# Attention and token-mixing MLP on one core: the order of instructions from a search over partial orders, with the dispatcher's tolerances set for each stretch of the program

## The chip, the cores and the metric

The kernel runs on one core of one Trainium2 chip. The metric is the device time in microseconds (us) of one execution. A core has five engines with a queue of instructions each: TensorE (PE in the profile; its weight loads are shown apart as PEld), VectorE (DVE), ScalarE (ACT), GpSimd (POOL) and SyncE (SP), which here issues DMAs. Each engine works its queue strictly in the order in which the program was written; across engines only semaphores order the work.

## The reference

The input is normalized once, and the result goes through a 32-head attention and through an MLP over the token axis; both are added to the input. Cut to what matters:

```python
S, D, H, Dh, F = 2048, 512, 32, 16, 1376
def _A_ref(x, wqkv, wo):
    q, k, v = split_heads(x @ wqkv)
    p = _softmax(einsum("bhqd,bhkd->bhqk", q, k) * Dh ** -0.5)
    return merge_heads(einsum("bhqk,bhkd->bhqd", p, v)) @ wo

def _B_ref(x, w1, b1, w2, b2):
    h = _layernorm(x)
    u = _gelu(einsum("bsd,sf->bdf", h, w1) + b1)
    return transpose(einsum("bdf,fs->bds", u, w2) + b2)

xn = _layernorm(A_x)
return A_x + _A_ref(xn, A_wqkv, A_wo) + _B_ref(xn, B_w1, B_b1, B_w2, B_b2)
```

The largest part by far is the softmax: 32 heads x 2048 x 2048 exponentials.

## The kernel before

**Tiling.** Attention is cut into 32 blocks (`NBLK`): 4 blocks of 512 queries times 8 sets of 4 heads. A block has 16 groups, one for each tile of 128 keys, 512 groups in all (`NGRP`). A group is 4 score rows, one for each head: a 128 x 512 tile of scores, which TensorE makes with one matmul (`score_mm`, L558) into one of eight PSUM banks. The 4 heads lie in 4 row groups of the array, so matmuls for different heads run side by side.

**Two ways to an exponential.** ScalarE takes two score rows at a time from a pair of banks (banks 0 and 1, or 2 and 3, by turns) with one exponential over 1024 columns into a buffer `pT` (`exp_tile`, L566); a group is two of those. VectorE makes its exponentials with integer arithmetic on the bits of a bf16: for each score row a first pass (`dve_first`, L613) from bank 4, 5 or 7 into a plane in SBUF, an add and a clamp; then two more planes for the whole group (`add_plane`, L618), each the first plane shifted by a constant. The three planes are summed by TensorE. So a group costs ScalarE two instructions, or VectorE six. Planes live in `plx` and in tiles that are done with (`x_sb`, `xn_sb`, part of `h_sb`, and others).

**PV.** `pv_mm` (L578) multiplies the exponentials by V and sums over the key tiles in bank 6; an extra column of ones gives the softmax's denominator. A PV bundle is 4 matmuls in 4 column groups of the array: one bundle for a group of ScalarE, three (one for each plane) for a group of VectorE. When a block's last bundle is done, its epilogue (`chain_epi`) copies bank 6 (L1095), takes the reciprocals (L1110) after a trip through DRAM, broadcasts them by DMA and multiplies on GpSimd (L1132). The last block has a shorter epilogue on VectorE (`tail_epilogue`: transposes L1737 and L1744), followed by its half of the output projection (L909) and four stores.

**Everything else** is cut into chains of steps: the projections of K, V and Q (L499), the MLP's first product (L860, with L871 to empty the bank), the GELU on ScalarE in the midst of the exponentials (L882, with two loads of activation tables), the MLP's second product with the output projection of finished blocks (L891, L901), and the normalizations. These matmuls use the full array and run in bank 7, 5 or 4 while no score row of VectorE is there.

**What sets the order.** Nothing is ordered by hand behind the ramp. A dispatcher runs on the host while the program is built: it keeps a planned clock for each engine (`Sched.add` adds a planned duration and end for each instruction, and 95 ns, `SWITCH`, when TensorE changes between score rows, PV columns and full-array matmuls) and asks the engine with the earliest clock for its next piece of work. That order becomes the engines' queues; semaphore waits are derived from the tiles read and written. On the chip nothing is decided again. `pe_step` chooses for TensorE:

- If ScalarE's next pair of banks is free within reach, it issues two score rows for it, and along with them score rows for VectorE into banks that are free within `JOIN` (80 ns).
- Otherwise it lets `pe_fill` issue a filler: a PV bundle, or the next full-array matmul of a chain. A filler may end up to `TOL` (115 ns) behind the moment at which ScalarE's banks come free.
- `DEFER` (250 ns) is how far it puts the score rows off so that a VectorE bank can come free and join them.
- If VectorE's backlog is under `D_HUNGRY` (0), or ScalarE's banks are over `FAR` (1300 ns) away, it issues score rows for VectorE alone.
- If fewer than `KEEP` (8) units of work stand in the last 3.4 us of the plan, it issues a matmul of zeros (L1579).

`dve_step` chooses for VectorE by priority: emptying a bank of a chain, first passes (`P1_PRI`, -1, when all three banks are taken), then planes (2). `D_PEND` (0) is how many score rows of VectorE's may be pending before another group is fetched. Which groups go to VectorE isn't fixed in advance; `d_pick1` gives it the next open group whenever score rows can be issued for it, so the split follows from the plan.

Of the kernel before, what the change touches and what calls it, by code (L numbers as in the profile page):

```python
# [1 line left out]

# [11 lines left out]
S = 2048  # L14
# [43 lines left out]
NPB = 8  # L58
# [25 lines left out]

SWITCH = 95.0


class Sched:  # L90
    ENGS = ("pe", "act", "dve", "pool", "sp")

    def __init__(self, nc, es):
        self.nc = nc
        self.es = es
        self.streams = {e: [] for e in self.ENGS}
        self.order = []
        self.last_writer = {}
        self.readers = {}
        self.dma_ops = []  # L100
        self.free = {e: 0.0 for e in self.ENGS}
        self.cfg = None
        self.busy = {e: 0.0 for e in self.ENGS}
        self.two = None
        self.wide = 0.0

    def ready(self, reads=(), writes=(), eng=None):
        t = 0.0
# [13 lines left out]
    def add(self, eng, fn, reads=(), writes=(), name="", dma=False, extra_deps=(), out_dma=False,  # L122
            occ=100.0, lat=None, cfg=None, two=False):
        op = Op(eng, fn, name)
        op.is_dma = dma
        op.q = "o" if out_dma else "i"
        deps = set()
        for k in reads:
            w = self.last_writer.get(k)
            if w is not None:  # L130
                deps.add(w)
            if k[0] == "bank":
                for r in self.readers.get(k, ()):
# [12 lines left out]
        if eng == "pe" and not dma:  # L146
            deps = {d for d in deps if d.eng != "pe" or d.is_dma}
        op.deps = list(deps)
        for k in reads:
            self.readers.setdefault(k, []).append(op)  # L150
        for k in writes:
            self.last_writer[k] = op
            self.readers[k] = []
        op.pos = len(self.streams[eng])
        self.streams[eng].append(op)
        self.order.append(op)
        if dma:
            self.dma_ops.append(op)
        t = self.free[eng]
        if cfg is not None:  # L160
            if self.cfg is not None and cfg != self.cfg:
                t += SWITCH
            self.cfg = cfg
        if eng == "pool" and self.two is not None:
            op.deps.append(self.two)
        for d in op.deps:
            t = max(t, d.end)
        if two:
            t = max(t, self.wide)
            self.two = op  # L170
        op.start = t
        op.occ = occ
        op.end = t + (lat if lat is not None else occ + 150.0)
        self.free[eng] = t + occ
        if eng == "pool" and occ > 1000.0:
            self.wide = t + occ
        self.busy[eng] += occ
        return op
# [79 lines left out]
def bass_parallel_sum__softmax_full_mha__mixer_token_mlp__prompt_kernel(  # L258
# [18 lines left out]
    with ExitStack() as es:  # L277
# [65 lines left out]
        def dma(q, dst, src, reads, writes, name="", noncontig=False, out_dma=False, lat=2500.0, move=150.0):  # L343
            if noncontig:
                def fn(eng, dst=dst, src=src):
                    with nc.allow_non_contiguous_dma(reason="small strided transfer"):
                        return eng.dma_start(dst, src)
            else:
                def fn(eng, dst=dst, src=src):
                    return eng.dma_start(dst, src)  # L350
            op = sc.add(q, fn, reads=reads, writes=writes, name=name, dma=True, out_dma=out_dma, occ=450.0, lat=lat)

            dma_free[0] = max(dma_free[0], op.start + 1300.0) + move
            op.end = max(op.end, dma_free[0] + 700.0)
            return op

        NPRE = 4
# [363 lines left out]
        plane_busy = {}  # L721
        pv_block = [0]
        pv_open = [True]
        kt_done = {0: 4}
        vt_done = {0: 4}
        k0_done = set(range(NPRE))
# [22 lines left out]
        class Chain:  # L749
# [6 lines left out]

            def pace(self):
                n = sum(s.eng == "pe" for s in self.steps)
                return self.rel + (self.due - self.rel) * self.i / n - 0.05

            def head(self):
                return self.steps[self.i] if self.i < len(self.steps) else None
# [678 lines left out]
                    bg[-1].t = sc.streams["pe"][-1].end  # L1441
                    bg[-1].due = -1.0

        TOL = 115.0
        JOIN = 80.0
        DEFER = 250.0
        P1_PRI = -1
        D_PEND = 0

        def pe_fill(t, lim, same_cfg):  # L1450
            cands = []
# [7 lines left out]
            for xb in (EX_BANK, 5, 4):  # L1459
# [15 lines left out]
                if ch is not None and ch.head().eng == "pe" and ch.t <= t:  # L1475
                    if rdy is None:
                        rdy = [c for c in ex_queue if c.rel <= st_["pos"] and (c.gate is None or c.gate())]
                    if any(c is not ch for c in rdy) or ch.pace() <= st_["pos"] or (early and xb != EX_BANK):
                        if not any(c[0] == "F" and ex_active[c[2]] is None for c in cands) or early:
                            cands.append(("F", ch, xb))  # L1480
                        late = late or ch.due < st_["pos"]
            order = []
            pv_press = len(buf_busy) >= NPB - 3 or len(planes_avail()) < 3
            for c in cands:
                same = 0 if c[0] == sc.cfg else 1
                if sc.cfg == "S" and n_unit(c, t) < 2:
                    same = 2
                if c[0] == "P":
                    order.append(((0 if pv_press else 1), same, 0.0, c))
                else:  # L1490
                    order.append(((0 if late else 1), same, c[1].due, c))
            order.sort(key=lambda z: z[:3])
            for _, _, _, c in order:
                if same_cfg and c[0] != sc.cfg:
# [110 lines left out]
        def act_left():  # L1605
            return sum(groups_open.values()) + len(act_cur[1])

        D_HUNGRY = 0.0
        PVM, PLM, PAM = 0.0, 0.0, 0.0
        FAR = 1300.0  # L1610
        n_act_ = [0]

        def chain_step(ch, t):
# [16 lines left out]
        def dve_step(t):  # L1630
# [20 lines left out]
            pool_on = sc.wide > t  # L1651
            for dg in d_groups:
                if dg["n1"] == 4 and dg["t"] <= t and not pool_on and plane_room(dg):
                    c.append((0.5 if closing(dg) else 2, dg["g"], lambda dg=dg: plane_step(dg)))
            if not c:
                return False
            min(c, key=lambda z: z[:2])[2]()
# [24 lines left out]
            return False  # L1682

        def wake_times(t):
            z = []
            for o in sc.order[-400:]:
                if o.end > t:
                    z.append(o.end)
                if o.start > t:
                    z.append(o.start)  # L1690
            for v in sc.free.values():
                if v > t:
                    z.append(v)
            return min(z) if z else None

        sc.free["sp"] = 0.0
        look = {e: sc.free[e] for e in ("pe", "dve", "pool", "sp")}
        guard = 0
        while True:
# [4 lines left out]
            if t > look[e]:  # L1704
                look[e] = t
                continue
            now[0] = t
            if e == "pe":
                did = pe_step(t)
            elif e == "dve":  # L1710
# [134 lines left out]
```

## Time and profile before

| | us |
|---|---|
| three runs | 696.21, 696.72, 697.99 (median 696.72) |
| the profiled execution | 697.93 |
| its span, first to last instruction | 696.1 |
| ScalarE busy | 679.5 |
| VectorE busy | 656.5 |
| TensorE busy (matmuls) | 655.3 |
| GpSimd busy | 66.3 |

The profile is that of one execution. Busy times count the stretches in which at least one instruction of an engine is under way; neighbours on an engine overlap, so the mean duration of an instruction is longer than what it adds to the end, and the pitch (from start to start) is the better price. "L566" is line 566 of the kernel before; the changed kernel has the same code further down (L566 is its L649, L558 its L641, L613 and L618 its L696 and L701, L578 its L661). DMA traffic is light: 41 GB/s from and to HBM over the span.

### The profile page before, as it was taken

The numbers are of one execution on the slowest core, as the hardware profiler recorded it, in microseconds if no ns is written. First come the engines' busy times: TensorE is split into PE (matmuls) and PEld (weight loads), VectorE is DVE, ScalarE is ACT, GpSimd is POOL, SyncE is SP. The second block draws the span as 40 slices with busy tenths as digits, with TensorE's granted clock in tenths as the row PEclk, the third lists the DMA queues.
The fourth block names the chain that finished last, engine by engine and source line by source line (L and its number), as shares of the span: only waits on it lengthen the run. The fifth ranks groups of instructions, "written<-read, shape, count | busy, mean of one in ns | idle before, by whom it ended". The sixth has DMA issues, their size and how long they took to land.

```text
span 696.1 us, 15540 instructions
## 1 busy us (share of the span) xinstructions
PE 655.3 (94%) x6195; PEld 199.7 (29%) x6281; DVE 656.5 (94%) x1139; ACT 679.5 (98%) x741; POOL 66.3 (10%) x94
## 2 busy tenths in 40 slices
PE   8999999999999999999999999998989999999987
PEld 4533333322222222222222222222222222222222
DVE  6988999999999999999999999999999999999997
ACT  5999999999999999999999999999999999999995
POOL 5520100000000000000000000000000000002000
PEclk9999999999999999999999999999999999999999
DMA  8042100112122312102221222211110022211001
GB/s 214 29 81 40 37 14 14 28 49 52 41 55 52 72 30 53 40 19 56 58 59 46 54 52 54 54 44 45 41 26 15 24 53 63 55 45 43 11 14 46
DMA packets 78431, 32.65 MB, mean 47 GB/s; under 512 B 63068, under 2 KB 74268, under 8 KB 78360
## 3 DMA queue, kind: packets, MB, share of 16 engines
q1 hardware_dynamic: 77512, 31.27, 18.5%
q8 instruction: 49, 0.80, 0.5%
q10 hardware_dynamic: 848, 0.39, 0.2%
q14 instruction: 22, 0.18, 0.1%
HBM read 26.08 MB, written 2.61 MB: 41 GB/s over the span
## 4 chain that ended last, share of the span: by engine, by line
ACT 85%; PE 10%; DVE 4%; issue 1%; DMA 0%; DVEq 0%; SPq 0%
ACT pT L566 83%; PE ps L558 3%; PE ps L578 3%; PE ps L891 1%; PE ps L499 1%; DVE x_sb L613 1%; ACT gT L882 1%; DVE stats L444 1%; PE ps L901 1%; PE ps L632 0%; DMA x_sb<-in_A_x_dram 0%; DVE plx L613 0%; DVE xnT L495 0%; DVE xn_sb L464 0%; PE ps L909 0%
## 5 line engine op out<-in xcount | busy, mean ns | idle before, releaser
L566 ACT ACTIVATE pT<-ps 128x1024 bf16<-128x1024 f32 x726 | 666.6, 1146 | 1.3 <-PE ps L558 0.9
L558 PE MATMUL ps<-QT,KT 32*128 32x512 bf16 x2048 | 289.2, 384 | 20.9 <-ACT pT L566 17.5
L613 DVE TENSOR_SCALAR x_sb<-ps 128x512 int16<-128x512 f32 x292 | 198.8, 683 | 14.2 <-PE ps L558 4.4
L613 DVE TENSOR_SCALAR plx<-ps 128x512 int16<-128x512 f32 x260 | 169.6, 679 | 1.3 <-PE ps L558 0.9
L558 PEld LDWEIGHTS ps<-QT,KT 32*128 32x128 bf16 x2048 | 73.4, 91 | 277.7 <-ACT pT L566 267.0
L578 PE MATMUL ps<-pT,V 128*32 128x512 bf16 x1452 | 142.8, 390 | 0.8 <-DVE OT L1095 0.4
L618 DVE TENSOR_SCALAR x_sb<-plx 128x2048 int16<-128x2048 int16 x88 | 59.7, 682 | 1.4 <-PE ps L578 0.8
L578 PEld LDWEIGHTS ps<-pT,V 128*32 128x32 bf16 x1452 | 36.2, 93 | 79.8 <-issue 75.0
L578 PE MATMUL ps<-x_sb,V 128*32 128x512 bf16 x580 | 56.0, 382 | 0.8 <-issue 0.5
L618 DVE TENSOR_SCALAR plx<-x_sb 128x2048 int16<-128x2048 int16 x74 | 50.5, 685 | 2.7 <-PE ps L578 2.5
L578 PE MATMUL ps<-plx,V 128*32 128x512 bf16 x544 | 52.8, 382 | 0.3 <-DVE plx L613 0.3
L1132 POOL TENSOR_TENSOR oT<-OT,denb 128x512 bf16<-128x512 f32 x16 | 20.3, 1268 | 340.5 <-DVE x_sb L618 166.0
L891 PE MATMUL ps<-gT,w2blk 128*128 128x512 bf16 (+1 forms) x150 | 48.2, 384 | 3.3 <-issue 2.9
L860 PE MATMUL ps<-h_sb,w1blk 128*128 128x512 bf16 (+1 forms) x158 | 47.9, 385 | 2.6 <-issue 2.2
L618 DVE TENSOR_SCALAR x_sb<-x_sb 128x2048 int16<-128x2048 int16 x65 | 44.1, 681 | 0.2
L1132 POOL TENSOR_TENSOR otmp<-OT,denb 128x512 bf16<-128x512 f32 x15 | 19.1, 1271 | 261.5 <-DVE x_sb L618 168.0
L499 PE MATMUL ps<-xnT,wqkv_sb 128*128 128x512 bf16 (+1 forms) x166 | 35.3, 309 | 3.0 <-issue 1.9
L578 PE MATMUL ps<-x_sb,V17b 128*32 128x512 bf16 x368 | 36.0, 382 | 0.2 <-DVE x_sb L618 0.2
L613 DVE TENSOR_SCALAR xn_sb<-ps 128x512 int16<-128x512 f32 x44 | 30.1, 683 | 2.1 <-PE ps L558 0.7
L618 DVE TENSOR_SCALAR plx<-plx 128x2048 int16<-128x2048 int16 x32 | 21.9, 685 | 1.2 <-PE ps L578 0.6
L499 PE MATMUL ps<-wqkv_sb,xnT 128*128 128x128 bf16 x256 | 21.2, 220 | 0.2 <-issue 0.2
L1095 DVE COPY OT<-ps 128x512 f32<-128x512 f32 x31 | 21.1, 680 | 0.0
(93 smaller groups left out, 355.1 us busy)
## 6 DMA issues: line engine op xcount, KB each, us to landing
denb<-rec_scr SPq DMA_DIRECT2D x124, 64.0 KB, 2.1
w1blk<-in_B_w_dram SPq DMA_DIRECT2D x10, 512.0 KB, 5.0
w2blk<-in_B_w_dram SPq DMA_DIRECT2D x16, 320.0 KB, 3.4
xres<-in_A_x_dram SPq DMA_DIRECT2D x16, 128.0 KB, 2.8
QT<-qst SPq DMA_DIRECT2D x120, 16.0 KB, 1.8
out_dram<-osb SPq DMA_DIRECT2D x14, 128.0 KB, 1.7
wqkv_sb<-in_A_wqkv_dram SPq DMA_DIRECT2D x3, 384.0 KB
x_sb<-in_A_x_dram SPq DMA_DIRECT2D x2, 512.0 KB, 6.5
```

What stands on the lines that cost most here:

```text
L444: sc.add("dve", lambda e: e.bn_stats(stats[:, t, :], x_sb[:, t, :]), reads=[("x", t), ("xh", t)], writes=[("stats", t)], occ=650, lat=780)
L499: return sc.add("pe", lambda e: e.matmul(dst, lhsT=lhsT, rhs=rhs, start=(ct == 0), stop=(ct == NCT - 1)), reads=reads, writes=[("bank", bk ...
L558: return sc.add("pe", lambda e: e.matmul(bank(bk), lhsT=KT[32 * r:32 * r + 32, T, 128 * kt:128 * (kt + 1)], rhs=QT[32 * r:32 * r + 32, slo ...
L566: return sc.add("act", lambda e: e.activation(pT[:, buf, :], ps[:, slot * 1024:(slot + 1) * 1024], ACTF.Exp, scale=EXP_SCALE), reads=[("ba ...
L578: return sc.add("pe", lambda e: e.matmul(bank(PV_BANK)[32 * r:32 * r + 32, :], lhsT=vt_[:, off:off + 32], rhs=rhs, start=start, stop=stop, ...
L613: return sc.add("dve", lambda e: e.tensor_scalar(plane_i[pb][:, 512 * r:512 * (r + 1)], bank(bk), BIAS, 0.0, ALU.add, ALU.max), reads=[("b ...
L618: return sc.add("dve", lambda e: e.tensor_scalar(plane_i[pb], plane_i[pb0], float(SHIFT[j]), BITS_MAX, ALU.add, ALU.min), reads=[("pl", pb ...
L860: op = sc.add("pe", lambda e: e.matmul(bank(xb)[0:m, :], lhsT=w1blk[:, slot, st, 0:m], rhs=h_sb[:, st, :], start=(st == 0), stop=(st == NT ...
L882: op = sc.add("act", lambda e, m=m, f0=f0, f1=f1: e.activation(gT[0:m, f0:f1, :], gT[0:m, f0:f1, :], ACTF.Gelu_apprx_tanh), reads=[("gT", ...
L891: op = sc.add("pe", lambda e: e.matmul(bank(xb), lhsT=w2blk[0:m, slot, ft, :], rhs=gT[0:m, ft, :], start=first, stop=last), reads=([("w2bl ...
L1095: op = sc.add("dve", lambda e: e.tensor_copy(OT32[:, eb, :], bank(PV_BANK)), reads=[("bank", PV_BANK)], writes=[("OT32", eb)], **T_DVE(512))
L1132: op = sc.add("pool", lambda e: e.tensor_tensor(dst, OT32[:, eb, :], denb[:, :], ALU.mult), reads=[("OT32", eb)] + [("denb", r) for r in r ...
```

## The change

The dispatcher's fixed numbers become a table, `POLICY`, with a row of eleven for each 10 us (`SEG`) of planned time. The main loop loads the next row when the planned clock passes its start; the last row, the 69th, stays to the end. The first three rows are the old numbers. Four numbers that stood in expressions are now in the table: `PACE` (0.05 before: how far ahead of its pace a chain may run), `N_SAME` (2: how many units must be at hand for a change of TensorE's mode to be taken gladly), `PRESS` (3: how few free buffers or planes make PV urgent) and `PL_PRI` (2: the priority of planes on VectorE; 0.9 puts them ahead of first passes while a bank is free).

```diff
+import heapq
+SEG = 10000.0
+POLICY = [
+    (115.0, 80.0, 250.0, -1, 0, 1300.0, 0.0, 0.05, 2, 3, 2),
...
+    (125.0, 80.0, 300.0, -1, 0, 900.0, 100.0, 0.05, 2, 4, 2),
+    (105.0, 60.0, 300.0, 1, 0, 2000.0, 300.0, 0.0, 2, 3, 2),
...
+    (130.0, 100.0, 150.0, 1, 0, 900.0, 0.0, 0.0, 2, 5, 2),
+]
@@ class Sched
+        self.marks = []
...
+        heapq.heappush(self.marks, op.start)
+        heapq.heappush(self.marks, op.end)
@@ Chain.pace
-                return self.rel + (self.due - self.rel) * self.i / n - 0.05
+                return self.rel + (self.due - self.rel) * self.i / n - PACE
@@ pe_fill
-                    if any(c is not ch for c in rdy) or ch.pace() <= st_["pos"] or (early and xb != EX_BANK):
+                    if BURST > 0 and ex_active[xb] is ch or any(c is not ch for c in rdy) or ch.pace() <= st_["pos"] or (early and xb != EX_BANK):
...
-            pv_press = len(buf_busy) >= NPB - 3 or len(planes_avail()) < 3
+            pv_press = len(buf_busy) >= NPB - PRESS or len(planes_avail()) < PRESS
...
-                if sc.cfg == "S" and n_unit(c, t) < 2:
+                if sc.cfg == "S" and n_unit(c, t) < N_SAME:
...
-                    order.append(((0 if late else 1), same, c[1].due, c))
+                    go = BURST > 1 and ex_active[c[2]] is not None
+                    order.append(((0 if late or go else 1), same, c[1].due, c))
@@ constants
-        TOL = 115.0
-        JOIN = 80.0
-        DEFER = 250.0
-        P1_PRI = -1
-        D_PEND = 0
...
-        D_HUNGRY = 0.0
+        BURST = 0
...
-        FAR = 1300.0
@@ dve_step
-                    c.append((0.5 if closing(dg) else 2, dg["g"], lambda dg=dg: plane_step(dg)))
+                    c.append((0.5 if closing(dg) else PL_PRI, dg["g"], lambda dg=dg: plane_step(dg)))
@@ wake_times
-            z = []
-            for o in sc.order[-400:]:
-                if o.end > t:
-                    z.append(o.end)
-                if o.start > t:
-                    z.append(o.start)
+            while sc.marks and sc.marks[0] <= t:
+                heapq.heappop(sc.marks)
+            z = sc.marks[:1]
@@ main loop
+            while n_seg[0] * SEG <= t:
+                TOL, JOIN, DEFER, P1_PRI, D_PEND, FAR, D_HUNGRY, PACE, N_SAME, PRESS, PL_PRI = POLICY[min(n_seg[0], len(POLICY) - 1)]
+                n_seg[0] += 1
```

`wake_times` gives the planned moment at which an idle engine is asked again; it now takes it from a heap of all planned starts and ends instead of from the last 400 instructions. `BURST` is 0, so the two expressions with it are as before. Over the table, `TOL` runs from 90 to 210 ns, `JOIN` from 30 to 100, `DEFER` from 150 to 450, `FAR` from 900 to 2000, `D_HUNGRY` over 0, 100 and 300, and `P1_PRI` is 1 in twelve rows, which lets planes that close a block go ahead of first passes.

The search itself, a beam over partial orders, isn't in the file: the table is what it left. The new program differs from the old in the order of instructions on all engines but GpSimd, and in the counts that follow from which groups went to VectorE:

| instructions | before | after |
|---|---|---|
| exponentials on ScalarE (L566) | 726 | 722 |
| first passes on VectorE (L613) | 596 | 604 |
| further planes on VectorE (L618) | 298 | 302 |
| PV matmuls (L578) | 3240 | 3256 |
| matmuls of zeros behind the ramp (L1579) | 49 | 41 |

More of the change, by code (lines that the diff above doesn't have):

```diff
@@ L354, in dma @@
             op.end = max(op.end, dma_free[0] + 700.0)
+            heapq.heappush(sc.marks, op.end)
             return op
@@ L723, in bass_parallel_sum__softmax_full_mha__mixer_token_mlp__prompt_kernel @@
         pv_open = [True]
+        TOL, JOIN, DEFER, P1_PRI, D_PEND, FAR, D_HUNGRY, PACE, N_SAME, PRESS, PL_PRI = POLICY[0]
         kt_done = {0: 4}
@@ L1696, in bass_parallel_sum__softmax_full_mha__mixer_token_mlp__prompt_kernel @@
         sc.free["sp"] = 0.0
+        n_seg = [0]
         look = {e: sc.free[e] for e in ("pe", "dve", "pool", "sp")}
```

65 rows, old and new, of the table POLICY are left out of this document.

## The prediction

> **What bounds the kernel now.** I read the page's head and chain first.
>
> ```profile
> span 696.1 us, 15540 instructions
> ...
> PE 655.3 (94%) x6195; PEld 199.7 (29%) x6281; DVE 656.5 (94%) x1139; ACT 679.5 (98%) x741; POOL 66.3 (10%) x94
> ...
> PEclk9999999999999999999999999999999999999999
> ...
> ACT 85%; PE 10%; DVE 4%; issue 1%; DMA 0%; DVEq 0%; SPq 0%
> ...
> L566 ACT ACTIVATE pT<-ps 128x1024 bf16<-128x1024 f32 x726 | 666.6, 1146 | 1.3 <-PE ps L558 0.9
> L558 PE MATMUL ps<-QT,KT 32*128 32x512 bf16 x2048 | 289.2, 384 | 20.9 <-ACT pT L566 17.5
> ```
>
> ScalarE is the bound: 98% busy, 85% of the chain, and 666.6 of its 679.5 us are one kind of work, the 726 exponentials. It stood idle before them for 1.3 us. 666.6 / 726 = 0.918 us is what one exponential adds to the end (the mean of 1.146 us overlaps with its neighbour). VectorE, which takes the groups of scores that ScalarE doesn't, shows the same 94% as TensorE. How much room each has between the ramp and the tail is read from the table by stretches:
>
> ```profile
> core 0: us, PE busy (x) PEld busy (x) DVE busy (x) ACT busy (x) POOL busy (x), PEclk, DMA share, GB/s
> ...
> 40.00:680.00 640.00, 607.90 (x5757) 177.18 (x5837) 614.40 (x1038) 639.73 (x694) 42.46 (x35) 1.00 0.18 43
> ```
>
> From 40 to 680 us ScalarE is busy for all but 0.3 us, VectorE leaves 640 - 614.4 = 25.6 us free, TensorE 32.1. So a shorter run needs fewer exponentials, or a closer pitch between them. For the closest pitch I took a stretch of ScalarE's timeline:
>
> ```profile
> start us, us, engine line op out<-in xcount [idle before <-releaser]
> 71.36 15.73 ACT L566 ACTIVATE pT<-ps 128x1024 bf16<-128x1024 f32 x17
> ```
>
> 17 exponentials in 15.73 us are 16 pitches and one full duration: (15.73 - 1.15) / 16 = 0.911 us. Between that and 0.918 lie 0.007 x 726, about 5 us, in which scores came late although the profile shows nearly no idle time. That is all a better order can win without dropping exponentials.
>
> **The change, part by part.** The rule for picking work keeps its form; the constants change with each 10 us of planned time. I therefore counted the two instruction streams.
>
> *Head.* TensorE's stream is the same up to the score rows of the first exponentials and ScalarE's up to the 25th exponential; the DMA queue's differs only behind its 95th entry, GpSimd's nowhere. Cost: 0, with no cover needed.
>
> *ScalarE.* 722 exponentials in place of 726: two of 512 groups go to VectorE (151, before 149). Two per group, 4 x 0.918 = -3.67 us. The page "ScalarE: Activation LUTs" of the Trainium skill (What ACT_TABLE_LOAD costs) has an activation with immediate scale at 186 ns + 0.833 ns an element, neighbours overlapping by about 93 ns. For 1024 elements that is an estimate of 946 ns, where this trace measures 918; by the page the four would be worth -3.8.
>
> *VectorE.* Each group costs four first passes (L613) and two further planes (L618): 12 instructions more. Their price is their pitch when nothing stops them:
>
> ```profile
> 404.30 0.68 DVE L613 TENSOR_SCALAR plx<-ps 128x512 int16<-128x512 f32 x1
> 404.90 0.68 DVE L618 TENSOR_SCALAR plx<-xn_sb 128x2048 int16<-128x2048 int16 x1
> 405.50 1.28 DVE L613 TENSOR_SCALAR plx<-ps 128x512 int16<-128x512 f32 x2
> ```
>
> Starts 0.60 us apart: 12 x 0.60 = 7.2 us. They lie beside ScalarE's exponentials, in the 25.6 us that VectorE has free, which leaves 18.4, 2.9% of the 640. With the cover wholly gone they cost +7.2; wholly hidden, 0. What a late VectorE does is seen near 518 us, on TensorE:
>
> ```profile
> 517.13 0.39 PE L558 MATMUL ps<-QT,KT 32*128 32x512 bf16 x3
> 517.45 0.40 PE L578 MATMUL ps<-pT,V 128*32 128x512 bf16 x4
> 517.68 0.39 PE L578 MATMUL ps<-x_sb,V17b 128*32 128x512 bf16 x4
> 518.00 0.65 PE L558 MATMUL ps<-QT,KT 32*128 32x512 bf16 x3
> 518.58 0.87 PE L578 MATMUL ps<-x_sb,V 128*32 128x512 bf16 x4
> 519.38 0.39 PE L558 MATMUL ps<-QT,KT 32*128 32x512 bf16 x3
> ```
>
> A regular step, from score rows to score rows with two fillers between, takes 518.00 - 517.13 = 0.87 us. In the next one a score row waits for a bank that VectorE has not read and a PV column for a plane; it takes 1.38, and the next exponential's rows stand behind both in TensorE's queue. How often TensorE waits at all is in the waits:
>
> ```profile
> engine line waited for: us in total, times, longest us
> PEld ps L558 <- ACT pT L566: 267.0, 670, 0.8
> ...
> PE ps L558 <- ACT pT L566: 17.5, 63, 0.5
> ...
> PEld ps L578 <- DVE plx L618: 3.9, 13, 0.4
> PEld ps L578 <- DVE OT L1095: 3.4, 11, 0.5
> ...
> PEld ps L578 <- DVE x_sb L618: 2.8, 11, 0.5
> ...
> PEld ps L558 <- DVE x_sb L613: 2.2, 7, 0.5
> ```
>
> Against 670 waits for ScalarE stand some forty for VectorE in the largest rows, 12 us, part of it absorbed before it reaches ScalarE. VectorE's free time falls by 7.2 / 25.6 = 28%; if these waits grow by the same 28%, 3.4 us, and a sixth of it gets through to ScalarE (the share I choose, nearest to the row of 1.3 us idle against 12 of waits), this is +0.5 us. Ends: 0 and +7.2.
>
> *TensorE.* Four PV bundles more (two groups give six where two were), eight zero matmuls fewer (41, before 49). The number of steps with three or more filler units between two exponentials' score rows falls from 134 to 116; changes between score rows, PV columns and full-array matmuls rise from 1520 to 1543. The first matters most, by these rows of the same engine:
>
> ```profile
> 403.37 0.39 PE L558 MATMUL ps<-QT,KT 32*128 32x512 bf16 x3
> 403.70 0.40 PE L578 MATMUL ps<-pT,V 128*32 128x512 bf16 x4
> 403.92 0.39 PE L578 MATMUL ps<-plx,V17b 128*32 128x512 bf16 x4
> 404.25 0.39 PE L558 MATMUL ps<-QT,KT 32*128 32x512 bf16 x3
> 404.57 0.82 PE L891 MATMUL ps<-gT,w2blk 128*128 128x512 bf16 x3
> 405.32 0.39 PE L558 MATMUL ps<-QT,KT 32*128 32x512 bf16 x3
> ```
>
> Two fillers: 0.88 us, inside one exponential. Three: 1.07, 0.15 longer than an exponential, covered only by what the score rows had in hand. If all 5 us of loose pitch came from the 134 long steps, each would cost 37 ns; 18 fewer give -0.67, which I take as -0.6. Bounds: 0, if the lateness has other causes, and -5, if it all goes. A mode change adds 404.25 - 403.92 - 0.22 = 0.11 us, 23 of them 2.5 us spread over the run; the eight zero matmuls and four PV bundles at 0.22 give back 0.9. TensorE's 17.5 us of waiting for ScalarE covers the rest; uncovered it is +1.6.
>
> *Tail.* In the kernel before, the last exponential isn't the last thing that PV waits for:
>
> ```profile
> 679.22 8.53 ACT L566 ACTIVATE pT<-ps 128x1024 bf16<-128x1024 f32 x9
> ```
>
> ```profile
> 687.81 0.40 PE L578 MATMUL ps<-plx,V 128*32 128x512 bf16 x4
> 688.04 0.39 PE L578 MATMUL ps<-pT,V 128*32 128x512 bf16 x4
> 688.25 0.39 PE L578 MATMUL ps<-x_sb,V17b 128*32 128x512 bf16 x4
> ```
>
> ```profile
> 688.70 0.72 DVE L1737 STREAM_TRANSPOSE denb<-ps 128x512 f32<-128x512 f32 x1 [0.64 <-PE ps L578]
> ```
>
> Exponentials end at 687.75, a VectorE plane's PV follows the last pT one, and the transpose starts at 688.70, 0.95 behind. In the changed stream the last PV bundle is that of the last exponential, and VectorE's planes are all read before its score rows. So the transpose starts 0.40 + 0.1 behind: -0.45 us, between 0 and -0.9. What moved ahead of that bundle are five full-array matmuls of the last output tiles. One (L909's counterpart) waits for GpSimd's product of the block before the last, the other queue that this step is moved past:
>
> ```profile
> L1132 POOL TENSOR_TENSOR oT<-OT,denb x16: 1264/1268/1274, 74.5 to 685.5; 128x512 bf16<-128x512 f32 x16
> ```
>
> It ends at 685.5 + 1.3 = 686.8, 0.95 ahead of the last exponential's end, and its reciprocal stands in VectorE's stream 11 instructions ahead of the transpose, before 15. If TensorE reaches it first, its wait delays the last bundle and the gain is the first thing lost; with 0.95 in hand I cost it at nothing. The chain behind the transpose has the same instructions.
>
> **Sum**, against the profiled execution (697.93 us, its span 696.1 and 1.8 around it): -3.67 + 0.5 - 0.6 - 0.45 = -4.2, so 693.7. That execution lies 1.2 above the median of 696.72; from the median it is 692.5.
>
> **The rivals.** *The order also closes the pitch* (A). Different tolerances for each stretch could remove most of the late score rows: 722 x 0.911 saves 5.1 of pitch on top of 3.67 and 0.45, so 687.5. For it: fewer long steps, so the plan moves that way. Against: 116 remain, and VectorE has less free time.
>
> *The gain is eaten* (B). VectorE's 2.9% of free time isn't where the groups are; waits like that of 518 us, where 1.38 - 0.92 = 0.46 us was lost, come nine times more often in the run: -4.2 - 0.5 + 9 x 0.46 = -0.6, so 696.1.
>
> *VectorE becomes the bound* (C, slower). With 151 groups, the free time is short in whole stretches; score rows for VectorE stand in TensorE's queue ahead of ScalarE's. From 11 further waits of 0.46 us on, the kernel is slower; at the full 7.2 us of added VectorE work on the path and the mode changes uncovered (+1.6) it is -3.67 + 7.2 + 1.6 = +5.1, so 701.8. For it: VectorE at 96% already in 40 to 680 us. Against: only 4.9 us of ScalarE's loose pitch now, with 149 groups at the same rule.
>
> *The clock drops* (D). TensorE's keep-warm zero matmuls fall by eight. The granted clock is 1.00 in every stretch above; slow matmuls of this case stand only at the start:
>
> ```profile
> L672 PE MATMUL ps<-KT,zw x12: 607/634/634, 1.3 to 7.8; 128*128 128x512 bf16 x12
> ```
>
> At 634 against 384 ns, one step of 0.87 becomes 1.44, half a microsecond lost each; over a stretch as long as that (6.5 us, some five steps at 1.44) about 2.6 us, so two such stretches give 697.7. Against: the rows put in their place are real work, and TensorE is 95% busy. The page "TensorE: Matmul & The Clock Gate" of the Trainium skill (What's actually happening) says the clock is halved after an idle window of about 3.4 us; no row here shows such a gap after the start.
>
> *The order doesn't change* (E): excluded by the two streams.
>
> **How the numbers follow.** Forecast (3 to 6 us faster) 0.52, A 0.10, B 0.16, C 0.19, D 0.03. What a measurement can tell from no change is 0.3%, 2.1 us. Faster by more: forecast, A and a fifth of B, 0.65; within: most of B and a share of C and D, 0.17; slower: the rest, 0.18. The range takes A's near half, B whole, and C up to +1.6 us: 689.0 to 698.3; the forecast's own is 690.7 to 693.7.
>
> **What would show it.** 722 exponentials, their idle time below 2 us and busy time near 662.8; a pitch of 0.917 to 0.919; VectorE's free time in the middle near 18 us; the first transpose half a microsecond behind the last exponential. I'm wrong if the pitch rises past 0.924 (then the four exponentials are given back), if waits on VectorE at L558's and L578's counterparts double, or if the granted clock falls anywhere.

## The result, and the profile after

| | before | after |
|---|---|---|
| median | 696.33 us (696.13 to 697.99, 6 runs) | 692.54 us (691.62 to 693.53, 6 runs) |
| ratio of after to before | | 0.9941, 95% interval 0.9928 to 0.9954 |
| profiled execution | 697.93 us, span 696.1 | 691.97 us, span 689.9 |

The changed kernel is 3.8 us faster; the forecast from the median was 4.2. Its page, with the lines that answer to those of before:

```profile
span 689.9 us, 15638 instructions
...
PE 668.5 (97%) x6289; PEld 198.3 (29%) x6289; DVE 659.3 (96%) x1151; ACT 675.5 (98%) x737; POOL 66.1 (10%) x94
...
PEclk9999999999999999999999999999999999999999
...
ACT 87%; PE 7%; DVE 4%; issue 1%; DMA 0%; DVEq 0%
...
L649 ACT ACTIVATE pT<-ps 128x1024 bf16<-128x1024 f32 x722 | 662.5, 1146 | 1.3 <-PE ps L641 1.2
```

ScalarE's 722 exponentials take 662.5 us, 4.1 less than the 726 before, at 0.918 us each again, with the same 1.3 us of idle time. The table by stretches, in the same columns as before:

```profile
40.00:680.00 640.00, 626.50 (x5907) 178.24 (x5906) 623.69 (x1058) 639.94 (x694) 42.69 (x36) 1.00 0.19 44
```

VectorE's free time between 40 and 680 us fell from 25.6 to 16.3 us; TensorE's seems to fall from 32.1 to 13.5. The second pair needs care. The profile of before holds 6195 records of matmuls beside 6281 of weight loads, that of after 6289 beside 6289: 86 matmul records are missing before. One group of full-array matmuls, which both programs issue 176 times, shows it on the page of before:

```profile
L891 PE MATMUL ps<-gT,w2blk 128*128 128x512 bf16 (+1 forms) x150 | 48.2, 384 | 3.3 <-issue 2.9
```

The profile of run 2 (below) has the order of the kernel before and all 6281 records. The same stretch there:

```profile
40.00:680.00 640.00, 623.55 (x5854) 177.41 (x5852) 615.39 (x1039) 635.49 (x696) 42.48 (x35) 1.00 0.18 43
```

So TensorE had some 16 us free before (16.5 here, 16.0 in run 3), not 32.1, and 13.5 after.

Whether VectorE's added work made TensorE wait is in the waits. The three largest rows in which PV matmuls of the changed kernel wait for VectorE:

```profile
PEld ps L661 <- DVE OT L1179: 3.9, 12, 0.5
...
PEld ps L661 <- DVE plx L696: 2.7, 11, 0.4
...
PEld ps L661 <- DVE x_sb L701: 2.0, 8, 0.3
```

They hold 8.6 us in 31 waits; the three largest before held 10.1 in 35. Over all rows in which the weight load of a score row or a PV matmul waits for a pass, a plane or the copy of bank 6, it is 15.3 us in 55 waits before and 14.5 in 56 after. These waits did not grow.

The end of the program, in ScalarE's, TensorE's and VectorE's timelines:

```profile
659.13 23.06 ACT L649 ACTIVATE pT<-ps 128x1024 bf16<-128x1024 f32 x25
```

```profile
681.21 0.60 PE L985 MATMUL ps<-wo_c,oT 128*128 128x512 bf16 x2
681.66 0.38 PE L993 MATMUL ps<-wo_pad,oT 128*128 128x512 bf16 x1
681.87 0.59 PE L1020 MATMUL ps<-xnT,ident 128*128 128x512 bf16 x2
682.40 0.40 PE L661 MATMUL ps<-pT,V 128*32 128x512 bf16 x4
...
685.12 1.04 PE L993 MATMUL ps<-wo_pad,otmp 128*128 128x512 bf16 x4
```

```profile
682.85 0.72 DVE L1817 STREAM_TRANSPOSE denb<-ps 128x512 f32<-128x512 f32 x1 [3.11 <-PE ps L661]
...
685.98 1.29 DVE L1835 TENSOR_TENSOR xres<-ps,h_sb 128x512 bf16<-128x512 f32 x2 [0.92 <-PE ps L993]
```

In the kernel before, the last matmuls (TensorE's timeline) and the last output sums (VectorE's) stand at:

```profile
691.39 1.03 PE L909 MATMUL ps<-wo_pad,otmp 128*128 128x512 bf16 x4
```

```profile
692.24 1.29 DVE L1755 TENSOR_TENSOR xres<-ps,h_sb 128x512 bf16<-128x512 f32 x2 [1.34 <-PE ps L909]
```

The last exponential ends at 682.19 and the span at 689.89, 7.70 behind; before it was 8.39. The transpose now starts 0.66 behind the last exponential (0.95 before), which is 0.29 of the 0.69. The other 0.40 comes from the five full-array matmuls that moved ahead of the last PV bundle: from the transpose to the last output sums it is 685.98 - 682.85 = 3.13 us, and 692.24 - 688.70 = 3.54 before, where TensorE was still working those matmuls off when VectorE's part was ready. That part ended at 690.90 us before, and the matmuls that read it began 0.49 us later; after, it ended at 685.06 and they began 0.06 us later.

The two profiled executions also differ where the programs do not: the first exponential starts at 12.28 us before and at 10.82 after. That is the ramp's scatter from run to run (last section), and it makes up 1.5 of the 6.2 us between this pair of spans. The medians, 3.8 us apart, appear to mix executions with a quick and with a slow ramp; they also hold the time outside the span, which varies from 1.8 to 2.6 us in the changed kernel's six runs.

### The profile page after: what moved, and what is told of

It reads as the page before. It is cut to its first block, busy times and chain, and to the rows that moved or that the text cites. A ratio compares the mean times of both kernels' runs of the same rounds, so it can differ in the third digit from the quotient of the medians.

```text
span 689.9 us, 15638 instructions
## 1 busy us (share of the span) xinstructions
PE 668.5 (97%) x6289; PEld 198.3 (29%) x6289; DVE 659.3 (96%) x1151; ACT 675.5 (98%) x737; POOL 66.1 (10%) x94
## 4 chain that ended last, share of the span: by engine, by line
ACT 87%; PE 7%; DVE 4%; issue 1%; DMA 0%; DVEq 0%
ACT pT L649 86%; PE ps L661 3%; PE ps L641 2%; DVE x_sb L696 1%; PE ps L582 1%; ACT gT L966 1%; DVE plx L701 1%; DVE plx L696 1%; PE ps L975 0%; DVE stats L527 0%; DVE xn_sb L696 0%; DMA x_sb<-in_A_x_dram 0%; PE ps L715 0%; PE ps L985 0%; PE ps L1659 0%
## 5 line engine op out<-in xcount | busy, mean ns | idle before, releaser
L649 ACT ACTIVATE pT<-ps 128x1024 bf16<-128x1024 f32 x722 | 662.5, 1146 | 1.3 <-PE ps L641 1.2
L641 PE MATMUL ps<-QT,KT 32*128 32x512 bf16 x2048 | 287.5, 384 | 13.0 <-ACT pT L649 10.5
L696 DVE TENSOR_SCALAR plx<-ps 128x512 int16<-128x512 f32 x324 | 213.5, 682 | 4.1 <-PE ps L641 3.2
L696 DVE TENSOR_SCALAR x_sb<-ps 128x512 int16<-128x512 f32 x212 | 144.4, 684 | 6.2 <-PE ps L641 0.5
L701 DVE TENSOR_SCALAR x_sb<-plx 128x2048 int16<-128x2048 int16 x128 | 87.1, 685 | 1.0 <-PE ps L661 0.7
L975 PE MATMUL ps<-gT,w2blk 128*128 128x512 bf16 (+1 forms) x176 | 56.7, 385 | 0.1
L661 PE MATMUL ps<-x_sb,V17b 128*32 128x512 bf16 x444 | 43.5, 383 | 0.0
L696 DVE TENSOR_SCALAR xn_sb<-ps 128x512 int16<-128x512 f32 x60 | 41.1, 685 | 2.2
L582 PE MATMUL ps<-xnT,wqkv_sb 128*128 128x512 bf16 (+1 forms) x188 | 41.6, 315 | 0.6 <-DVE xnT L578 0.4
L701 DVE TENSOR_SCALAR x_sb<-x_sb 128x2048 int16<-128x2048 int16 x52 | 35.4, 683 | 0.0
L701 DVE TENSOR_SCALAR plx<-x_sb 128x2048 int16<-128x2048 int16 x41 | 28.0, 685 | 0.2
L975 PEld LDWEIGHTS ps<-gT,w2blk 128*128 128x128 bf16 (+1 forms) x176 | 13.1, 97 | 26.9 <-issue 22.3
```

Source lines behind the costliest of these rows:

```text
L582: return sc.add("pe", lambda e: e.matmul(dst, lhsT=lhsT, rhs=rhs, start=(ct == 0), stop=(ct == NCT - 1)), reads=reads, writes=[("bank", bk ...
L641: return sc.add("pe", lambda e: e.matmul(bank(bk), lhsT=KT[32 * r:32 * r + 32, T, 128 * kt:128 * (kt + 1)], rhs=QT[32 * r:32 * r + 32, slo ...
L649: return sc.add("act", lambda e: e.activation(pT[:, buf, :], ps[:, slot * 1024:(slot + 1) * 1024], ACTF.Exp, scale=EXP_SCALE), reads=[("ba ...
L661: return sc.add("pe", lambda e: e.matmul(bank(PV_BANK)[32 * r:32 * r + 32, :], lhsT=vt_[:, off:off + 32], rhs=rhs, start=start, stop=stop, ...
L696: return sc.add("dve", lambda e: e.tensor_scalar(plane_i[pb][:, 512 * r:512 * (r + 1)], bank(bk), BIAS, 0.0, ALU.add, ALU.max), reads=[("b ...
L701: return sc.add("dve", lambda e: e.tensor_scalar(plane_i[pb], plane_i[pb0], float(SHIFT[j]), BITS_MAX, ALU.add, ALU.min), reads=[("pl", pb ...
```

## Experiments

Ratios are to the kernel before, in the same runs; the changed kernel's is 0.9941.

**1. The old numbers in the new code.** With all 69 rows at the old numbers, the built program is the kernel before instruction for instruction, on all engines and with the same waits. This is read from the two built programs, without a run on the chip. So the heap in `wake_times` and the new names change nothing by themselves, and all that follows is the table.

**2. Eight exponentials made short, order untouched** (in the kernel before).

```diff
-  e.activation(pT[:, buf, :], ps[:, slot * 1024:(slot + 1) * 1024], ACTF.Exp, scale=EXP_SCALE)
+  n = 1 if n_exp[0] % 80 == 60 and n_exp[0] < 640 else 1024
+  e.activation(pT[:, buf, 0:n], ps[:, slot * 1024:slot * 1024 + n], ACTF.Exp, scale=EXP_SCALE)
```

> The kernel before with its order untouched; eight of the 726 exponentials, evenly spread, work on 1 column instead of 1024 (the rest of those buffers is left out). Theory 'ScalarE's work sets the end': an activation of one column took 0.20 us in the ramp, an exponential adds 0.918, so eight save about 8 x 0.7 = 5.7 us: some 690.6, ratio 0.992. Rival 'VectorE bounds as well': VectorE's work is unchanged, so less than half comes through, 693.5 or more. Rival 'the gain of the changed kernel is its order, not its count': no more than 1 us.

Measured: 695.52 us, ratio 0.9987 (0.9978 to 0.9996), 1.1 us less than the kernel before in the same runs (696.59). ScalarE's work did fall, and became idle time (busy, mean, idle before):

```profile
L570 ACT ACTIVATE pT<-ps 128x1024 bf16<-128x1024 f32 x726 | 661.2, 1120 | 5.5 <-PE ps L558 5.4
```

Where it went is seen behind the short exponential at 287.3 us, in the timeline of all engines:

```profile
286.87 0.39 PE L558 MATMUL ps<-QT,KT 32*128 32x512 bf16 x3
...
287.74 0.39 PE L558 MATMUL ps<-QT,KT 32*128 32x512 bf16 x3
...
288.17 2.96 ACT L570 ACTIVATE pT<-ps 128x1024 bf16<-128x1024 f32 x3 [0.61 <-PE ps L558]
...
288.60 0.39 PE L558 MATMUL ps<-QT,KT 32*128 32x512 bf16 x3
```

The next score rows come 0.87 us behind the last ones, as in every step with two fillers: TensorE's queue holds the fillers that were planned for a full exponential. ScalarE waits 0.61 us for them, and 0.92 - 0.87 is all that is won at this place. My theory of ScalarE as the one bound falls: in a fixed order TensorE's steps pace the kernel nearly as closely. By its time alone the run would also fit the rival of VectorE; but all but 0.1 of the 5.5 us of idle time end with TensorE's score rows, and at this place no wait for VectorE stands ahead of them.

**3. and 4. Twelve VectorE instructions more, order untouched** (in both kernels; planned duration 0, so that the plan stays).

```diff
   op = add_plane(j, dg["pl"][0], dg["pl"][j])
+  n_plane[0] += 1
+  if n_plane[0] % 22 == 0 and 11 < n_plane[0] < 276:
+      sc.add("dve", lambda e: e.bn_stats(spare[:, :], KT[:, 0, 0:512]), ..., occ=0.0, lat=0.0)
```

> The kernel before with its order untouched and 12 more VectorE instructions of about 0.61 us (statistics of 512 columns of K into a spare tile) behind every 22nd further plane: the 7.3 us of VectorE work that the change adds, without its four exponentials fewer. Theory 'hidden in VectorE's free time': +0 to +0.8, 696.3 to 697.1. Rival 'VectorE bounds as well': half or more of 7.3, so 700 or above.

> The same 12 VectorE instructions in the changed kernel, whose VectorE has 16.3 us free between 40 and 680 us instead of 25.6. Theory 'hidden': +0.3 to +1.5, 692.8 to 694.0, a little more than in the kernel before because less is free. Rival 'the change has used up VectorE': +4 or more, 696.5 or above.

Measured: 701.45 us in the kernel before, ratio 1.0070 (1.0055 to 1.0085), and 696.92 us in the changed one, ratio 1.0005 (0.9995 to 1.0014). That is 701.45 - 696.59 = 4.9 and 696.92 - 692.54 = 4.4 us for 12 x 0.60 = 7.2 us of work. In both the rival holds: VectorE's 25.6 us of free time did not hide it. Nor was the changed kernel, with less free time, any more sensitive. How one of the delays travels, in the kernel before with the twelve, by the timeline of all engines:

```profile
304.28 0.68 DVE L1675 BATCH_NORM_STATS2 spare<-KT 128x6 f32<-128x512 bf16 x1
...
304.88 1.27 DVE L614 TENSOR_SCALAR plx<-ps 128x512 int16<-128x512 f32 x2
...
305.61 0.39 PE L559 MATMUL ps<-QT,KT 32*128 32x512 bf16 x1 [0.20 <-DVE plx L614]
...
305.93 0.85 PE L861 MATMUL ps<-h_sb,w1blk 128*96 128x512 bf16 x3
...
306.71 0.39 PE L559 MATMUL ps<-QT,KT 32*128 32x512 bf16 x3
...
307.14 1.94 ACT L567 ACTIVATE pT<-ps 128x1024 bf16<-128x1024 f32 x2 [0.36 <-PE ps L559]
```

The added instruction (L1675) puts two first passes back by 0.60 us, so a bank comes free late; the one score row that needs it waits on TensorE until 305.61, three fillers and ScalarE's own score rows (306.71) stand behind it in the queue, and ScalarE is idle for 0.36 us.

**5. ScalarE work added, order untouched** (in the changed kernel).

```diff
+  if n_exp[0] % 80 == 60 and n_exp[0] < 640:
+      sc.add("act", lambda e: e.activation(spare[:, :], KT[:, 0, 0:384], ACTF.Exp, scale=0.001), ..., occ=0.0, lat=0.0)
```

> The changed kernel with its order untouched and eight more ScalarE instructions, spread like the eight of the first run: an exponential of 384 columns into a spare tile, about 0.41 us each by the pitch of 1024 columns (0.186 + 0.833 x 0.384 by no row of this case; 0.903 x 384 / 1024 = 0.34 at least), 2.7 to 3.3 us in all. Theory 'ScalarE paces every step': all of it comes through, 695.2 to 695.8. Rival 'TensorE's steps pace as well, ScalarE catches up between long steps': half or less, below 694.

Measured: 695.62 us, ratio 0.9991 (0.9980 to 1.0002), 3.1 us more than the changed kernel. One of the eight in ScalarE's timeline:

```profile
67.31 0.66 ACT L654 ACTIVATE spare<-KT 128x384 bf16<-128x384 bf16 x1
67.73 2.08 ACT L656 ACTIVATE pT<-ps 128x1024 bf16<-128x1024 f32 x2
```

It delays the next exponential by 0.42 us; eight of that are 3.3, and nine tenths of it reach the end, as the first theory had it.

**6. VectorE work taken away, order untouched** (in the changed kernel).

```diff
+  m = 8 if n_plane[0] % 22 == 0 and 11 < n_plane[0] < 276 else 2048
-  e.tensor_scalar(plane_i[pb], plane_i[pb0], ...)
+  e.tensor_scalar(plane_i[pb][:, 0:m], plane_i[pb0][:, 0:m], ...)
```

> The changed kernel with its order untouched; 12 of its 302 further planes work on 8 columns instead of 2048 (the rest of those planes is left out), some 0.5 us less VectorE work each, 6 us in all. Theory 'in a fixed order a saving does not pay, only an addition does': 0 to -0.7, 691.8 to 692.5. Rival 'VectorE bounds': -3 or more, 689.5 or below.

Measured: 693.02 us, ratio 0.9945 (0.9930 to 0.9960): nothing won, though VectorE's busy time fell by 4.4 us (659.3 to 654.9). Runs 2 to 6 say the same in both directions: in a fixed order, work added to either engine cost most of its length (4.9 and 4.4 of 7.2 us, 3.1 of 3.3), and work taken away gained little (1.1 us of the 5.4 that ScalarE's busy time fell in run 2, nothing here).

**7. The zeros made small, order untouched** (in the changed kernel).

```diff
-  e.matmul(bank(PV_BANK), lhsT=zw[:], rhs=KT[:, 0, 0:512], start=first, stop=first)
+  e.matmul(bank(PV_BANK)[:, 0:8], lhsT=zw[:], rhs=KT[:, 0, 0:8], start=first, stop=first)
```

> The changed kernel with its order untouched; the 41 matmuls of zeros behind the ramp work on 8 columns instead of 512, so they no longer load the array. Theory 'the clock doesn't need them here': 0, within 0.7 us of 692.5, granted clock 1.00. Rival 'fewer zeros let the clock fall': granted clock below 1.00 in some stretch, and 2.6 us or more for each dip.

Measured: 699.68 us (695.82 to 701.38 in 10 runs), ratio 1.0032 (1.0012 to 1.0052), 7.1 us more than the changed kernel. By stretches, the last three columns being granted clock, DMA share and GB/s:

```profile
470.00:480.00 10.00, 8.74 (x83) 2.61 (x75) 10.00 (x18) 10.00 (x12) 1.26 (x1) 0.96 0.31 77
480.00:485.00 5.00, 4.81 (x30) 1.07 (x27) 4.48 (x8) 4.33 (x6) 0.00 (x0) 0.50 0.00 0
485.00:490.00 5.00, 5.00 (x39) 0.87 (x40) 3.44 (x7) 4.02 (x5) 0.00 (x0) 0.50 0.04 7
490.00:495.00 5.00, 5.00 (x52) 1.13 (x44) 3.95 (x8) 3.95 (x5) 0.00 (x0) 0.72 0.00 0
```

The clock falls to half for more than 10 us, with TensorE busy for 8.74 of the 10 us up to 480. It falls five times in this execution. So the zeros that remain in the changed kernel are needed. Why eight fewer than before are enough was not tried by itself.

**8. Other tables: is it the number of exponentials, or the order?** Four tables that mix old and new rows, and a fifth planned anew.

```diff
+POLICY = POLICY[:66] + [DEF] * 3                            # until66; DEF: the old numbers
+POLICY = [DEF[:9] + p[9:10] + DEF[10:] for p in POLICY]     # only PRESS new
+POLICY = [DEF] * 40 + POLICY[40:]                           # from row 40
+POLICY = [p[:6] + DEF[6:7] + p[7:] for p in POLICY]         # D_HUNGRY at 0
-    occ=917.0, lat=1080.0                                   # exp_tile: planned anew, 25 other rows
+    occ=903.0, lat=1080.0
```

> The changed kernel with the old numbers in the table's last three rows. 720 exponentials, the fewest of all, but 30 filler units instead of 21 stand behind the last score rows of ScalarE. Theory 'the number of exponentials sets the end': 2 x 0.918 less than the changed kernel, 690.7, or up to 693 if the longer tail takes part of it back. Rival 'planned clock' (the dispatcher's planned end, 2.2 us later than the changed kernel's, carries over to the chip): 694.8.

> The old numbers everywhere except PRESS, which keeps its row-by-row values. 726 exponentials as in the kernel before, fewer steps with three or more fillers (111, before 132) and 42 matmuls of zeros. Theory 'the number sets the end': as before, 696.3 within 0.7. Theory 'fewer long steps pay too': 0.5 to 1 less, 695.5. Rival 'planned clock' (1.6 us later than before): 697.9.

> The old numbers in the first 40 rows, the new ones behind: the same rows, but they now meet another order than the one they were chosen on. 730 exponentials. Theory 'the number sets the end': 4 x 0.918 more than before, 700.0. Rival 'planned clock' (2.9 us later than before): 699.2. Rival 'the new rows are better in themselves': faster than before.

> The changed kernel with D_HUNGRY at its old 0 in all rows, the other ten numbers new. 732 exponentials. Theory 'the number sets the end': 6 x 0.918 more than before, 701.8. Rival 'planned clock' (6.4 us later than before): 702.7. Rival 'the tolerances as such make the gain': between the two kernels, about 694.

> The changed kernel planned anew: the dispatcher counts an exponential as 903 ns (the closest pitch in the traces) instead of 917, and 25 of the 69 rows of the table are other numbers, found by a search on the new planned end. 730 exponentials, but 81 steps with three or more fillers instead of 114. Theory 'number times pitch plus tail': the pitch falls by what 33 long steps of some 50 ns cost, to 0.915, so 8 x 0.917 - 1.7 = +5.6 against the changed kernel, 698.2; at the closest pitch anywhere, 0.911, it is 695.3. Rival 'planned clock' (1.5 us earlier than the changed kernel's): 691.

| kernel | exponentials | busy + idle for each, us | tail, us | median, us | ratio (95%) |
|---|---|---|---|---|---|
| before | 726 | 0.920 | 8.4 | 696.33 | |
| after | 722 | 0.919 | 7.7 | 692.54 | 0.9941 (0.9928, 0.9954) |
| until66 | 720 | 0.920 | 11.9 | 694.72 | 0.9977 (0.9963, 0.9991) |
| only PRESS new | 726 | 0.925 | 8.6 | 700.19 | 1.0052 (1.0035, 1.0068) |
| from row 40 | 730 | 0.920 | 7.7 | 700.16 | 1.0048 (1.0032, 1.0065) |
| D_HUNGRY at 0 | 732 | 0.922 | 8.4 | 703.07 | 1.0088 (1.0071, 1.0105) |
| planned anew at 903 | 730 | 0.920 | 7.6 | 700.81 | 1.0059 (1.0039, 1.0079) |

The third column is the exponentials' busy time and the idle time before them, by their number; "tail" runs from the end of the last exponential to the end of the span. The ratios are to the kernel before in the same runs: its median was 696.83 beside until66 to D_HUNGRY, 696.30 beside the fifth. The exponentials' rows, in the table's order from until66 on, each from its own kernel:

```profile
L653 ACT ACTIVATE pT<-ps 128x1024 bf16<-128x1024 f32 x720 | 660.8, 1144 | 1.4 <-PE ps L645 1.2
```

```profile
L653 ACT ACTIVATE pT<-ps 128x1024 bf16<-128x1024 f32 x726 | 667.4, 1133 | 3.8 <-PE ps L645 3.6
```

```profile
L653 ACT ACTIVATE pT<-ps 128x1024 bf16<-128x1024 f32 x730 | 670.2, 1136 | 1.2 <-PE ps L645 0.9
```

```profile
L653 ACT ACTIVATE pT<-ps 128x1024 bf16<-128x1024 f32 x732 | 672.4, 1125 | 2.5 <-PE ps L645 2.4
```

```profile
L649 ACT ACTIVATE pT<-ps 128x1024 bf16<-128x1024 f32 x730 | 670.0, 1180 | 1.9 <-PE ps L641 1.6
```

Number times price, plus tail, gives each time from the changed kernel's within 1.3 us: for the fifth, 730 x 0.920 - 722 x 0.919 = 8.1 and 0.1 off the tail, so 700.5 against 700.81. This adds up one execution's profile; it does not say why a table has its number or its price. Neither the number alone nor its price alone gives the times. until66 has the fewest exponentials and is slower than the changed kernel, through its end:

```profile
675.90 4.69 ACT L653 ACTIVATE pT<-ps 128x1024 bf16<-128x1024 f32 x5
```

```profile
681.65 2.12 DVE L705 TENSOR_SCALAR plx<-x_sb 128x2048 int16<-128x2048 int16 x3
...
685.46 0.72 DVE L1821 STREAM_TRANSPOSE denb<-ps 128x512 f32<-128x512 f32 x1 [0.83 <-PE ps L665]
```

ScalarE is done at 680.59, but VectorE still makes planes of the last block, and the transpose starts 4.9 us behind (0.66 in the changed kernel). The two exponentials saved are lost twice over. And "only PRESS new" has the number of before and is 3.4 us slower than the kernel before in the same runs, through its price. One place of it, by stretches:

```profile
525.00:529.00 4.00, 3.43 (x38) 1.01 (x34) 3.94 (x7) 4.00 (x5) 0.00 (x0) 1.00 0.00 0
529.00:531.00 2.00, 1.28 (x15) 0.32 (x11) 1.97 (x4) 2.00 (x4) 0.00 (x0) 1.00 0.00 0
531.00:533.00 2.00, 2.00 (x16) 0.33 (x15) 1.90 (x4) 1.94 (x3) 0.00 (x0) 0.50 0.01 4
533.00:535.00 2.00, 2.00 (x22) 0.50 (x18) 1.27 (x2) 1.22 (x2) 0.00 (x0) 0.65 0.04 4
```

The order leaves TensorE short of work for a few microseconds, the clock halves, and two exponentials come late, by 0.50 and 0.45 us. The same place in TensorE's timeline:

```profile
530.33 0.39 PE L645 MATMUL ps<-QT,KT 32*128 32x512 bf16 x3 [0.53 <-ACT pT L653]
```

The longest hole there is 0.53 us. Not all of the price is the clock: ScalarE's longest wait behind the ramp, 0.80 us at 370 us, stands behind a step with seven fillers, with the clock at 1.00. The kernel planned anew has only 81 steps with three or more fillers instead of 114 (the prediction's 116 without the two of the ramp), and its price was to fall to 0.915; it stayed. The theory of the number met from row 40 (700.0 against 700.16) and came near D_HUNGRY at 0 (701.8 against 703.07), but missed until66 (690.7 to 693 against 694.72), only PRESS (696.3 against 700.19) and the fifth (698.2 against 700.81). The rival of the planned clock, which takes a table's time from its planned end, met until66 (694.8 against 694.72) and came near D_HUNGRY at 0 (702.7) and from row 40 (699.2), but missed only PRESS by 2.3 us and the fifth by 9.8: what bringing the planned end forward is worth is not in that number either. The changed kernel remains the fastest of all.

**9. The ramp's three zeros made small** (in the changed kernel; 8 columns in place of 512 in the `zeros(3, 330)` between the first and the second transposes).

> The changed kernel with its order untouched; the three matmuls of zeros between the first and the second tile's transposes of the ramp work on 8 columns instead of 512. In the profiled execution before they stood in front of the second tile's transposes (1.28 us) and the first exponential began at 12.28 us, in the changed one at 10.82. Theory 'the ramp's start varies by those three': the first exponential at 10.8 or earlier in every run, runs of one kind, median 692.0 to 692.5. Rival 'they are needed to warm the clock': slower matmuls in the ramp, first exponential at 11.5 or later, 693 or more.

Measured: 693.52 us, ratio 0.9954 (0.9938 to 0.9971). Stretches of that kernel:

```profile
5.00:10.00 5.00, 2.60 (x30) 2.48 (x30) 3.72 (x11) 1.78 (x5) 3.81 (x7) 0.81 0.96 262
10.00:15.00 5.00, 5.00 (x51) 3.36 (x50) 3.52 (x9) 4.03 (x7) 2.62 (x5) 0.85 1.07 338
```

The granted clock falls to 0.81 and 0.85 (1.00 in the changed kernel's profile), and the first exponential starts at 12.50 us. The first four transposes, at 6.56 us, still take 0.40 us; from 8.60 us on four take 0.63. So the rival holds: without the three the clock falls again in the ramp. A late start alone would prove little, since ramps with the three whole sometimes start nearly as late (last section); the fall of the clock is what shows it. Part of the lateness has another cause, the input, which landed at 5.20 us here and at 3.21 in the changed kernel's profile: the first transposes start 0.31 us later. In five of the six runs the mean granted clock is 0.995 to 0.997; the sixth, the slowest (695.41), shows 1.000 and is not explained.

## Why the prediction was right, step by step

- *The sum, -4.2*: the profiled pair gives -3.67 - 0.4 - 0.69 = -4.8 without the ramp, the medians -3.8. That 692.5 met 692.54 is in part luck: it was counted from a median of three runs, 696.72, where six gave 696.33, and the terms behind it were off, as follows.
- *ScalarE, -3.67*: right. The exponentials take 4.1 us less by the page, 3.67 of it their number at 0.918.
- *TensorE's closer pitch, -0.6, and VectorE's waits, +0.5*: together -0.1, measured -0.4 (the rest of the 4.1). The net was near; the reasons behind the two were not right. TensorE's waits for VectorE were to grow by 28%; they went from 15.3 to 14.5 us, so no run shows the +0.5. I costed VectorE's 7.2 us as hidden in its free time. Runs 3 and 4 show that the same amount put into a finished order costs 4.4 to 4.9 us: the free time is not cover, it is the waits of a queue in step with two others. That it cost nothing in the change I put down to the order made anew around it; the waits that did not grow fit this, but no run separates it. The "sixth" of the waits that I let through has no support either. That fewer long steps close the pitch is shown neither way: the fifth table of run 8 has 33 fewer and the same price.
- *TensorE's 32.1 us of free time*: wrong, a gap in the records, and so are its 94% busy (97% in run 2) and part of the 17.5 us of waiting for ScalarE that I took as cover (12.4 in run 2, 10.5 after). With some 16 us free before and 13.5 after, TensorE was the second bound, as run 2 shows.
- *Tail, -0.45*: -0.69. The part at the last PV bundle was 0.29; the five matmuls ahead of it, which I costed at nothing, brought the other 0.40, and GpSimd's product was not late.
- *Rival A* (a much closer pitch) did not happen: 0.918 stayed 0.918. *Rivals B and C* (VectorE) did not in this order: the waits did not grow, though VectorE's free time fell further than forecast (16.3 us, where I had 18.4). *Rival D* (the clock) I rated too low at 0.03: the mechanism is real (runs 7, 8 and 9). In one of the changed kernel's six runs, the slowest at 693.53, the granted clock is 0.997, in line with such a dip; single runs of the kernel before show 0.998 too.

## What to carry to other kernels

Where a host-side planner fixes the order of several nearly full engines, free time in the profile was no cover here: work added to a finished order cost most of its length and work removed gained little, so an edit should be costed with the order made anew, by counting the new streams. Price such a plan by three numbers: how many instructions of the pacing engine, what each adds, and what stands behind the last one. A better number in one of them says little alone: of five other tables none beat the changed one, and one with two exponentials fewer was slower.

## What the runs showed of the hardware

- The granted clock fell without any long gap in TensorE's work. Ahead of the dip in "only PRESS new" TensorE was busy 4.71 of 6 us; before the one in run 7, 8.74 of 10. The page "TensorE: Matmul & The Clock Gate" of the Trainium skill (What's actually happening) puts the halved clock behind an idle window of about 3.4 us. Read as a gap without matmuls, that does not stand here: the longest holes are 0.53 and 0.45 us. The measurement decides: thin work was enough. What made it too thin, the holes or the matmuls on a part of the array, the runs do not separate.
- A dip is dear: from 480 to 495 us of run 7 ScalarE is busy 4.33 + 4.02 + 3.95 = 12.3 of 15 us, so one dip costs the engine that paces the kernel 2.7 us.
- The ramp scatters from run to run with the same head. ScalarE's first exponentials, in its timeline of before and then of after:

```profile
12.28 2.85 ACT L566 ACTIVATE pT<-ps 128x1024 bf16<-128x1024 f32 x3
```

```profile
10.82 4.69 ACT L649 ACTIVATE pT<-ps 128x1024 bf16<-128x1024 f32 x5
```

  TensorE's timeline shows why. The ramp's three zero matmuls and the second transposes, in before and then in after:

```profile
6.98 1.49 PE L672 MATMUL ps<-KT,zw 128*128 128x512 bf16 x3
8.26 0.63 PE L632 MATMUL ps<-ident,xn_sb 128*128 128x128 bf16 x4
```

```profile
6.48 0.81 PE L755 MATMUL ps<-KT,zw 128*128 128x512 bf16 x3
7.58 0.40 PE L715 MATMUL ps<-ident,xn_sb 128*128 128x128 bf16 x4 [0.28 <-DVE xn_sb L547]
```

  In before the same matmuls run at about half the speed, as they do at a granted clock of 0.50 in "only PRESS new" (there a PV bundle takes 0.62 us, and 0.40 at 1.00). The granted-clock column does not show it: it reads 1.00 up to 15 us in both. Of the 13 profiles in which the three zeros are whole, nine have these transposes at 0.40 us and their first exponential between 10.71 and 11.29 us, and four have them at 0.63 and it between 11.92 and 12.28. When the input landed does not decide it: at 5.37 us in one of the nine, at 3.18 in one of the four. Ten runs of the kernel before in one set lie at 696.09 to 696.38 or at 697.27 to 697.89, some 1 to 1.5 us apart, which fits the two kinds of ramp. Why TensorE's clock comes up late in some executions was not tried.
